# A memory-augmented attention chain with swapped weights: weight loads issued at even steps of TensorE's program, and stores, x and left-row transfers placed behind them in SyncE's program

## The chip, the cores and the metric

The kernel is written for one Trainium2 chip and uses one of its cores. A core has TensorE (matrix products, shown as PE, its weight loads as PEld), VectorE (DVE), ScalarE (ACT), GpSimd (POOL) and SyncE (SP), and 16 DMA engines that move data between HBM and the on-chip memory. Each engine runs its own list of instructions in order and waits on semaphores. The metric is the device time of one execution in microseconds; three runs of the kernel before took 1645.34, 1648.09 and 1649.2 us (median 1648.09).

## The reference

A sequence of 2048 tokens of width 640 goes through attention in 64 segments of 32 tokens, one after the other, because each segment hands 8 memory rows to the next. Beside it the same tokens go through a gated feed-forward block, and a gate mixes the two. Cut to what matters:

```python
for s in range(n_seg):                      # 64 segments of 32 tokens
    h = concatenate([mem, x[s]])            # 8 memory rows + 32 tokens
    q, k, v = h @ Wq, h @ Wk, h @ Wv        # 640 -> 32 heads of 192, each
    p = softmax(where(mask, q @ k.T * scale, -1e9))
    o = (p @ v) @ Wo                        # 32*192 -> 640
    mem = o[:8]
    outs.append(o[8:])
a = concatenate(outs)
b = (gelu(x @ w_gate) * (x @ w_up)) @ w_down
out = g * a + (1 - g) * b                   # g = sigmoid((x * gate_w).sum(-1))
```

## The kernel before, in words

The feed-forward block runs first and leaves its result in a scratch tensor in HBM. Then come the 64 segments. All lists of instructions are recorded by a small scheduler: `add` notes for each operation which earlier operations it must wait for (by the memory regions that it reads and writes), and each engine runs its operations in the order in which they were recorded. DMAs of this stage are all issued by SyncE.

**Segments.** A segment's work on TensorE is written out by hand in `PROG` (or `PROG1`, `PROG3`, by q = s mod 4): `("g", i, k)` is step k of 5 of group i of the projections, `sc`, `ex`, `pt`, `pv` are scores, softmax, transposition and product with V for one octet (a quarter of the heads), `wo` the output projection, `lf` and `vb` projections of "left rows". Of a segment's 32 tokens the first 24 and the 8 memory rows go through the projections as one block of 32; the last 8 tokens of four segments in a row make a block of their own, the left rows, which is projected ahead of time (a group of four segments has the number g).

**Weights.** The projection weights stand in pieces of 384 KB (a matrix, an octet, a step k; 60 pieces) and 480 KB (16 pieces of Wo). They don't all fit on the chip, so 16 slots hold two pieces in turn. Even segments use the octets in the order 0, 1, 2, 3, odd ones in the order 3, 2, 1, 0. A segment uses the pieces of its first octet in these slots and then loads over them those of its last octet, which it uses near its end and the next segment uses at its beginning. Of these 16 loads 12 are for Q, K and V (two of Q, five of K, five of V), 3 for Wo, and one piece of Q has a path of its own (L1459 copies it out of the way first).

**Where loads are issued.** After each item of the program `swap_loads` looks at the pieces that the item has used (`done_keys`) and records at once the load of the partner of each (`load_piece`, L635). The load waits for the last TensorE operation that reads the old piece. As the pieces of the first octet are used by groups 0 and 1, the 12 loads stand in SyncE's list close behind each other, and the three of Wo behind the two halves of `("wo", 0)`.

**What else SyncE issues in a segment.** `out_store` (L1029) writes the finished rows of the segment before, `x_load` (L743) reads the tokens of the next one, `bz_load` (L1018) reads the feed-forward result into the buffer that `out_store` has emptied, `stg_load` (L1005) reads projected left rows. In segments with q = 0, `outl_store` (L1072) writes the left rows of the group before in two parcels of four small DMAs; in segments with q = 2, `bzl_load` (L1024) reads the feed-forward result for left rows, also in two parcels of four. The scheduler holds that a later write of the same output rows waits for the earlier one: the four rows of segments that `outl_store` covers lie within those of `out_store`, the last of which is the one that is issued in the same segment (q = 0). `bz_load` waits for the landing of `out_store`, since it fills the same buffer. At the end of a segment POOL scales that buffer (L1085, `mix`) and DVE adds the attention's result (L1087).

**Places.** Before the change, `out_store` stands behind `("g", 0, 3)` where q = 0 and behind `("g", 1, 4)` otherwise, `x_load` behind `("g", 1, 4)`; the first parcel of `outl_store` and `bzl_load` stands behind `("g", 1, 4)`, the second behind `("pv", 2)`.

Of the kernel before, what the change touches and what calls it, by code (L numbers as in the profile page):

```python
# [238 lines left out]
def _build(nc, A_x, A_mem0, A_Wq, A_Wk, A_Wv, A_Wo, seg_len, w_gate, w_up, w_down,  # L239
# [9 lines left out]
    KT = Dm // 128  # L249
# [3 lines left out]
    NOCT = NT // 4  # L253
# [20 lines left out]
    S_ = _Sched(nc)  # L274
# [354 lines left out]
    later = []  # L629

    loaded = {}

    def load_piece(key, name):
        loaded[slot_id[key]] = key
# [3 lines left out]
    def piece(seg, key):  # L638
        order = orders[seg % 4]
        oi = last_req.get(seg, -1) + 1  # L640
        assert order[oi] == key, "pieces must be consumed in order"
        last_req[seg] = oi
        if seg == 0 and key in tmp_off:
            return left_piece(key)
        if seg and key == (EM, octet(seg, 0), EK):
            return None, None
        done_keys.append(key)
        return piece_view(key, res_off[key]), r_res[key]

    def swap_loads(seg, item):  # L650
        if item[:2] == ("g", 0) and EK <= item[2] < KT - 1:
            later.extend(key for key in done_keys if key[0] == 1)
            done_keys[:] = [key for key in done_keys if key[0] != 1]
        elif later:
            done_keys[:] = sorted(done_keys + later, key=lambda key: key[:1] + key[2:])
            del later[:]
        for key in done_keys:
            other = swap_in.get(key)
            if other is None or (other in partner) == (seg % 2 == 0):
                continue  # L660
            load_piece(other, "swap s%d" % seg)
        del done_keys[:]

    def left_piece(key):
        if key in tmp_off:
# [796 lines left out]
    def segment(s):  # L1462
        g, q = s // 4, s % 4
        post = []
        n_wo, nqkv = n_wos[q], nqkvs[q]
        for n, item in enumerate(PROGS[q]):
            kind, i = item[0], item[1]
            if kind == "g":
                proj(s, item)
                if item == ("g", 0, EK):  # L1470
                    left_fill(s, 0)
                    if s:
                        S_.add("pool", lambda e: e.memset(Qz[0:64], 0.0), writes=[r_Qz], name="Qz zero s%d" % s)
                        S_.add("pool", lambda e: e.memset(pl_sb, 0.0), writes=[r_p], name="pl zero s%d" % s)
                ki = [j for m, j in GROUPS[i] if m == 1 and item[2] == KT - 1]
                kind, i = ("k", ki[0]) if ki else ("", 0)
            elif kind == "tq":
                row_transp(s, 0, i)
            elif kind == "tk":
                row_transp(s, 1, i)  # L1480
            elif kind == "sc":
                scores(s, i)
            elif kind == "ex":
                softmax(s, i)
            elif kind == "pt":
                p_transp(s, i)
            elif kind == "pv":
                pv_oct(s, i)
                if i == NOCT - 1 and q < 3:
                    half_sums(OB, "s%d" % s)  # L1490
            elif kind == "lf":
                if i == q and unit(s, item[2]):
                    if item[3] == 0:
                        for m in range(2):
                            lb[item[2], m] = misc_bank(s)
                    for m in range(2):
                        LBK[m] = lb[item[2], m]
                    left_mm(*unit(s, item[2]), item[3], unit_piece)
            elif kind == "vb":
                if q == 3 and g + 1 < NG:  # L1500
                    if i == 0:
                        lb["v"] = misc_bank(s)
                    vl_mm(s + 1, i)
            elif kind == "le":
                if i == q and unit(s, item[2]):
                    if n > n_wo:
                        post.append(item[2:])
                    else:
                        left_evac(s, *item[2:])
            else:  # L1510
                if q == 3:
                    wo_both(s, item)
                else:
                    wo_part(s, item)
            swap_loads(s, item)
            if item == ("g", 0, KT - 2):
                for x in to_store:
                    left_store(*x)
                del to_store[:]
                if s and q == 0:  # L1520
                    out_store(s - 1)
            if item == ("g", 1, KT - 1):
                if q:
                    out_store(s - 1)
                if s + 1 < NSEG:
                    x_load(s + 1)
            if item == ("sc", NOCT - 1) and s + 1 < NSEG:
                ek_copy(s, (0, 1))
                ek_copy(s, (2,))
            if item == ("pv", NOCT - 1) and q == 3 and s + 1 < NSEG:  # L1530
                mix_left_b(g)
            if item == ("pv", NOCT - 1) and q == 1:
                stg_load(s + 1, 1)
            if n == ek_at[q]:
                if s + 1 < NSEG:
                    if q != 1:
                        stg_load(s + 1, 0)
                    key = (EM, octet(s, NOCT - 1), EK)
                    load_piece(swap_in[key], "swap s%d" % s)
                    stg_load(s + 1, int(q != 1))  # L1540
            if s == 0 and item == ("g", 0, KT - 1):
                load_residents(3, lambda key: key[0] < 3 and on_tmp(key))
            if s == 0 and item == late_at:
                load_residents(3, lambda key: key[0] == 3)
            if item == ("wo", 0, 1):
                for x in mid_later:
                    mid_store(x)
                del mid_later[:]
                if s + 1 < NSEG:
                    bz_load(s)  # L1550
                else:
                    end_load()
                    end_gates()
                if q == 1 and g + 2 < NG:
                    xl_load(g + 2)
            if item in (("g", 1, KT - 1), ("pv", NOCT - 2)):
                js = (0, 1) if item[0] == "g" else (2, 3)
                if q == 0 and g > 0:
                    outl_store(g - 1, js)
                if q == 2 and g + 1 < NG:  # L1560
                    bzl_load(g, js)
            if n == nqkv and s + 1 < NSEG:
                x_copy(s + 1)
        if s + 1 == NSEG:
            end_store()
            return
        kv = [x.rearrange("p (c k) -> p c k", k=KT) for x in (Zt, ps[:, OB2, SC:512], zsum)]
        if q == 3:
            for j in (0, 2, 1, 3):
                dst, src = Zt[32 * j:32 * j + 32], ps[64 * (j // 2):64 * (j // 2) + 32, LB, DJ * (j % 2):DJ * (j % 2 + 1)]  # L1570
                if j < 2:
                    S_.add("dve", lambda e, dst=dst, src=src: e.tensor_copy(out=dst, in_=src),
                           reads=[r_lbq[0]], writes=[r_PTq[j]], name="Zq evac s%d" % s)
                else:
                    S_.add("act", lambda e, dst=dst, src=src: e.activation(out=dst, in_=src, func=ACTF.Copy),
                           reads=[r_lbq[2]], writes=[r_PTq[j]], name="Zq evac s%d" % s)
        for i in range(2):
            ka, kb = KA[i], KA[i + 1]
            if q < 3:
                S_.add("dve", lambda e, ka=ka, kb=kb: e.tensor_tensor(  # L1580
                    out=kv[0][:, :, ka:kb], in0=kv[1][:, :, ka:kb], in1=kv[2][:, :, ka:kb], op=ALU.add),
                    reads=[r_ps[OB2], r_zp[0]], writes=[r_Z[i]] + ([r_PT] if i == 0 else []), name="Z%s evac s%d" % ("a" if i == 0 else "", s))
            S_.add("dve", lambda e, ka=ka, kb=kb: e.transpose(  # L1583
                out=XB4[:, :, ka:kb, XA:L].rearrange("p g k i -> p k g i"), in_=kv[0][:, :, ka:kb].rearrange("p c k -> p k c")),
                reads=[r_Z[i]] + (r_PTq if q == 3 else []), writes=[r_Hm[i], r_Qm, r_Ql], name="Tm%d s%d" % (i, s))
        mix(s)
        if q == 3:
            left_sums(g)
        if "v" in lb:
            tick[0] += 1  # L1590
            misc[lb["v"]] = tick[0]
            vl_evac(s + 1, octet(s + 1, 0), lb.pop("v"), "act")
        for i in post:
            left_evac(s, *i)
# [82 lines left out]
```

## Time and profile before

| | |
|---|---|
| device time, median of 3 runs (lowest to highest) | 1648.09 us (1645.34 to 1649.2) |
| profiled execution, first to last instruction (its span, the only time that it has) | 2114.2 us |
| TensorE clock granted in it | 0.654 of full speed |
| bytes moved by DMA | 499.28 MB, mean 236 GB/s |
| busy: TensorE, VectorE, ScalarE, GpSimd | 99%, 48%, 38%, 26% of the span |
| swapped weights: loads of L635 by SyncE, Wk, Wv, Wq, Wo | 335, 335, 209, 205 |

The profile is one execution, taken apart from the timed runs, and it is longer than they are. Its rows give an engine, a line of the program, an operation, what it writes and reads, how many and how long; "out<-in" names tensors (`arena` is the on-chip memory, `ps` the accumulators). In a time line a row is a run of equal instructions: start, length, count. SyncE's rows (SPq) are the issuing of DMAs, not their transfer; the time to landing is given apart, where the trace has it.

### The profile page before, as it was taken

What the parts mean: (1) busy time and instruction counts of PE and PEld (TensorE: products, weight loads), DVE (VectorE), ACT (ScalarE), POOL (GpSimd) and SP (SyncE); (2) the same over time, 40 slices, a digit from 0 to 9 for tenths busy, and PEclk for the clock granted to TensorE, in tenths of its full rate; (3) what the DMA queues carried; (4) which work ended last, traced back from release to release, by engine and by line L of the source; (5) the groups of instructions that cost most, each with busy time, mean ns of one, the idle gap of its engine ahead of it and who ended that gap; (6) DMA issues with size and microseconds to landing.
All of it is one profiled execution on the core that took longest, in us unless ns stands there. A gap on an engine that the chain in (4) does not pass through costs nothing.

```text
span 2114.2 us, 75845 instructions
## 1 busy us (share of the span) xinstructions
PE 2098.0 (99%) x37107; PEld 958.1 (45%) x28147; DVE 1005.8 (48%) x3039; ACT 792.9 (38%) x1890; POOL 553.3 (26%) x1625
## 2 busy tenths in 40 slices
PE   9999999999999999999999999999999999999997
PEld 3444344444444444444444444444444444444444
DVE  4233254554545454545545454545455454545453
ACT  1111244343434343444434343434444343434342
POOL 1000023232232223232222323232322223222332
PEclk6666666666666666666666666666666666666666
DMA  9612577776768777677767677776777676777775
GB/s 319 182 33 57 184 268 260 248 270 232 253 219 275 244 258 241 227 255 254 274 233 249 221 268 249 255 251 225 248 256 270 239 258 212 261 256 249 254 264 174
DMA packets 275415, 499.28 MB, mean 236 GB/s; under 512 B 121119, under 2 KB 136327, under 8 KB 275079
## 3 DMA queue, kind: packets, MB, share of 16 engines
q1 hardware_dynamic: 271000, 491.30, 68.8%
q8 instruction: 255, 4.18, 0.8%
q10 hardware_dynamic: 4079, 3.14, 0.5%
q14 instruction: 81, 0.66, 0.1%
HBM read 473.25 MB, written 21.09 MB: 234 GB/s over the span
## 4 chain that ended last, share of the span: by engine, by line
PE 99%; DMA 0%; DVE 0%; SPq 0%; POOL 0%; ACT 0%; issue 0%; ACTq 0%; POOLq 0%; DVEq 0%
PE ps L226 26%; PE ps L1138 25%; PE ps L1338 9%; PE ps L1383 8%; PE ps L1282 4%; PE ps L930 4%; PE ps L839 4%; PE ps L836 4%; PE ps L862 3%; PE ps L1364 3%; PE ps L1187 2%; PE ps L1284 2%; PE ps L234 1%; PE ps L1195 1%; PE ps L971 1%; PE ps L1254 1%
## 5 line engine op out<-in xcount | busy, mean ns | idle before, releaser
L226 PE MATMUL ps<-arena 128*32 128x384 bf16 x8960 | 887.8, 430 | 0.4 <-ACT arena L1159 0.4
L1138 PE MATMUL ps<-arena 128*32 128x384 bf16 x8640 | 857.5, 420 | 2.0 <-DVE arena L1583 2.0
L1138 PEld LDWEIGHTS ps<-arena 128*32 128x32 bf16 x8640 | 303.3, 117 | 525.3 <-issue 379.7
L1176 DVE STREAM_TRANSPOSE arena<-arena 128x384 bf16<-128x384 bf16 x512 | 276.5, 562 | 144.1 <-ACT arena L1159 144.1
L1159 ACT ACTIVATE arena<-ps 128x384 bf16<-128x384 f32 x512 | 230.0, 491 | 160.1 <-PE ps L1138 160.1
L1214 DVE TENSOR_REDUCE arena<-ps 104x4 f32<-104x160 f32 x256 | 83.0, 324 | 340.2 <-PE ps L1202 340.2
L1338 PE MATMUL ps<-arena 128*32 128x320 bf16 x3456 | 241.0, 404 | 0.0
L1012 POOL COPY arena<-arena 128x96 bf16<-128x96 bf16 x256 | 70.2, 274 | 475.3 <-PE ps L1202 311.4
L1267 ACT ACTIVATE arena<-ps 128x448 bf16<-128x448 f32 x192 | 104.4, 544 | 237.7 <-PE ps L1254 233.3
L1179 POOL COPY arena<-arena 64x160 bf16<-64x160 bf16 x256 | 81.9, 320 | 385.5 <-DVE arena L1176 384.3
L1162 ACT ACTIVATE arena<-ps 128x384 bf16<-128x384 f32 x256 | 125.2, 489 | 128.1 <-PE ps L1138 127.5
L1383 PE MATMUL ps<-arena 128*64 128x320 bf16 x1536 | 169.6, 387 | 0.0
L1226 ACT ACTIVATE ps<-ps 104x160 f32<-104x160 f32 x256 | 74.8, 292 | 239.5 <-DVE ps L1216 239.5
L1320 ACT ACTIVATE arena<-ps 128x480 bf16<-128x480 f32 x192 | 109.5, 570 | 93.8 <-PE ps L1284 85.7
L930 PE MATMUL ps<-arena 128*32 128x384 bf16 x1280 | 142.5, 408 | 0.0
L1338 PEld LDWEIGHTS ps<-arena 128*32 128x32 bf16 x3456 | 113.3, 129 | 56.9 <-ACT arena L1261 18.1
L1282 PE MATMUL ps<-arena 128*64 128x160 bf16 x1536 | 135.2, 263 | 0.0
L1284 PE MATMUL ps<-arena 128*64 128x64 bf16 x1536 | 128.6, 225 | 0.0
L1228 DVE TENSOR_REDUCE arena<-ps 104x4 f32<-104x160 f32 x256 | 81.8, 319 | 88.4 <-ACT ps L1226 87.4
L1383 PEld LDWEIGHTS ps<-arena 128*64 128x64 bf16 x1536 | 93.2, 127 | 49.4 <-issue 9.6
L1282 PEld LDWEIGHTS ps<-arena 128*64 128x64 bf16 x1536 | 94.1, 126 | 42.8 <-ACT arena L1159 23.0
L1411 ACT ACTIVATE arena<-ps 128x384 bf16<-128x384 f32 x120 | 57.3, 491 | 123.9 <-DVE arena L1580 74.0
(102 smaller groups left out, 2518.2 us busy)
## 6 DMA issues: line engine op xcount, KB each, us to landing
arena<-in_A_Wk_dram SPq DMA_DIRECT2D x335, 384.0 KB, 5.8
arena<-in_A_Wv_dram SPq DMA_DIRECT2D x335, 384.0 KB, 8.4
arena<-in_A_Wo_dram SPq DMA_DIRECT2D x205, 480.0 KB, 4.3
arena<-in_A_Wq_dram SPq DMA_DIRECT2D x209, 384.0 KB, 4.8
arena<-left_qk_scratch SPq DMA_DIRECT2D x126, 96.0 KB, 3.9
left_qk_scratch<-arena SPq DMA_DIRECT2D x49, 192.0 KB, 4.6
left_qk_scratch<-arena SPq DMA_DIRECT2D x30, 96.0 KB, 3.7
ffn_b_scratch<-arena ACTq DMA_DIRECT2D x16, 160.0 KB, 2.3
```

What stands on the lines that cost most here:

```text
L226: return e.add_instruction(mybir.InstMatmult(name=nm, start_tensor_calc=like["start"], stop_tensor_calc=stop, tile_size=(128, 32), tile_po ...
L930: fns.append(lambda e, outp=outp, rhs=rhs, j=j: e.matmul(outp, lhs, rhs, start=(k == 0), stop=(k == KT - 1), tile_position=(0, 32 * j)))
L1138: fns.append(lambda e, outp=outp, rhs=rhs, j=j: e.matmul(outp, lhs, rhs, start=(k == 0), stop=(k == KT - 1), tile_position=(0, 32 * j)))
L1159: S_.add("act", lambda e, m=m, bk=bk: e.activation(out=rows_sb[m], in_=ps[:, bk, 0:384], func=ACTF.Copy), reads=[r_ps[bk]], writes=[r_rows ...
L1162: S_.add("act", lambda e, i=i, bk=bk: e.activation(out=v_sb[i % NVB].rearrange("p (c n) -> p c n", c=3), in_=ps[:, bk, 0:384].rearrange("p ...
L1176: S_.add("dve", lambda e: e.transpose(out=dst[:, :, 0:L], in_=rows_sb[m].rearrange("p (c r) -> p c r", r=L)), reads=[r_rows[m]], writes=[r ...
L1267: S_.add("act", lambda e: e.activation(out=PT, in_=ps[:, bank, 0:PTW + 128], func=ACTF.Copy), reads=[r_ps[bank]], writes=[r_PT], name="pT ...
L1282: return [lambda e: e.matmul(full, v[:, e0:e0 + 64], PTm[:, i], start=True, stop=False, tile_position=(0, 64 * i), skip_group_check=True), ...
L1284: lambda e: e.matmul(part, vl[:, e0:e0 + 64], PTl[:, i], start=False, stop=True, tile_position=(0, 64 * i), skip_group_check=True)]
L1320: S_.add("act", lambda e: e.activation(out=apx(u[:, 0, 0, :], [[rs, na], [3 * rs, 4], [1, R]]), in_=ps[:, A, 0:na * W].rearrange("p (c t r ...
L1338: fns.append(lambda e, i=i, t=t, j=j, gv=gv: e.matmul(ps[32 * j:32 * j + 32, bank, 0:2 * DJ].rearrange("p (h n) -> p h n", h=2), lhs2[i], ...
L1383: S_.add("pe", [lambda e, i=i, g_=g_, c=c, p=p, u=u: e.matmul(ps[64 * i:64 * i + 64, LB, 0:2 * DJ], u[:, c, :], g_[:, c, 2 * DJ * i:2 * DJ ...
```

## The change

The diff moves no operation of TensorE, VectorE, ScalarE or GpSimd; what differs is the place of SyncE's DMAs in its list and what the swapped loads wait for.

- A piece whose partner is to be loaded goes into a list `pend`. A clock adds up a duration for each item of TensorE's program (`item_ns`: 162 ns for a projection piece, 405 for an item of `wo`, and so on), and a load is taken from the list at most every 900 of these nanoseconds (`next_load`), or when its piece is needed.
- Each such load also waits for the TensorE operation that was recorded last when it was taken from the list.
- `out_store` of the segment before and `x_load` of the next stand behind `("sc", 2)`, for every q.
- The first parcel of `outl_store` (q = 0) and of `bzl_load` (q = 2) stands behind `("g", 4, 4)`.

```diff
+    pend, clock, SPACE = [], [0, 0], 900
...
     def piece(seg, key):
...
+        while key in pend:
+            next_load(seg)
         done_keys.append(key)
...
     def swap_loads(seg, item):
...
-            load_piece(other, "swap s%d" % seg)
+            pend.append(other)
         del done_keys[:]
+        clock[0] += item_ns(seg, item)
+        while pend and clock[0] >= clock[1]:
+            next_load(seg)
+
+    def next_load(seg):
+        load_piece(pend.pop(0), "swap s%d" % seg)
+        S_.streams["sp"][-1].deps.add(S_.streams["pe"][-1])
+        clock[1] = max(clock[1], clock[0] - SPACE) + SPACE
+
+    def item_ns(seg, item):
+        q = seg % 4
+        if item[0] == "g":
+            return 162 * (len(GROUPS[item[1]]) + int(q == 0 and any(m == 2 and i for m, i in GROUPS[item[1]])))
+        if item[0] == "lf":
+            return 325 if item[1] == q else 0
+        if item[0] == "wo":
+            return 810 if q == 3 else 405
+        return {"sc": 470, "pv": 500, "pt": 100, "vb": 162}.get(item[0], 0)
...
-                if s and q == 0:
-                    out_store(s - 1)
-            if item == ("g", 1, KT - 1):
-                if q:
+            if item == ("sc", 2):
+                if s:
                     out_store(s - 1)
                 if s + 1 < NSEG:
                     x_load(s + 1)
...
-            if item in (("g", 1, KT - 1), ("pv", NOCT - 2)):
+            if item in (("g", 4, KT - 1), ("pv", NOCT - 2)):
```

In SyncE's list of a segment with q = 0 the order around the three Wo pieces was: 12 pieces of Q, K and V with `out_store` after the third, `x_load`, four `outl_store`, three pieces of Wo, `bz_load`, `stg_load`, the single piece of Q, `stg_load`, four `outl_store`. After the change it is: 12 pieces, `out_store`, `x_load`, two pieces of Wo, four `outl_store`, the third piece of Wo, `bz_load`, and then as before. With q = 2 the same holds for `bzl_load`. With q = 1 and 3 the order is unchanged but for the places in time.

## The prediction

> **What bounds the kernel now.** I read the head of the page, the cores' clock and TensorE's own waits first.
>
> ```profile
> span 2114.2 us, 75845 instructions
> PE 2098.0 (99%) x37107; PEld 958.1 (45%) x28147; DVE 1005.8 (48%) x3039; ACT 792.9 (38%) x1890; POOL 553.3 (26%) x1625
> ...
> core 0: 2114.2 us, clock 0.654
> ...
> PE ps L836 <- DMA arena<-in_B_w_gate_dram: 0.4, 1, 0.4
> ```
>
> TensorE is busy for 99% of the span, and in the whole list of its waits a DMA stands once, with 0.4 us, for the first weights of the feed-forward block. In this execution the kernel is bound by TensorE alone, at a granted clock of 0.654, and no swapped piece is ever late.
>
> The timed runs are something else: their median, 1648.09 us, is 0.78 of the span. TensorE's 2098.0 us at 0.654 are 1372 us at full clock, so the timed runs had a granted clock between 1372/1648 = 0.83 (if TensorE never waits) and 1 (if 276 us are waits, 4.3 us for each of 64 segments). The trace cannot say where between. I therefore do the sum twice: at the trace's own times, and for the timed runs, where I let all marks of TensorE come at 0.78 of their distance from the segment's start, while DMA transfers and SyncE's issuing keep their lengths.
>
> [...]
>
> Then the DMA side: two stretches of a segment with q = 0 (the burst of 12 loads, the rest), a stretch within a burst, times to landing by issue, those of all L635, the ns (min/median/max) that issuing a piece of Wo takes, and one of SyncE's own waits.
>
> ```profile
> 1182.80:1199.10 16.30, 16.30 (x320) 5.57 (x198) 8.28 (x25) 6.11 (x16) 3.24 (x12) 0.65 0.85 298
> 1199.10:1212.30 13.20, 13.20 (x298) 7.86 (x270) 6.83 (x24) 4.75 (x12) 4.68 (x12) 0.65 0.51 164
> ...
> 1015.00:1023.00 8.00, 8.00 (x158) 2.31 (x82) 4.95 (x16) 4.09 (x10) 1.92 (x7) 0.65 1.04 413
> ...
> arena<-in_A_Wv_dram SPq DMA_DIRECT2D x335, 384.0 KB, 8.4
> arena<-in_A_Wo_dram SPq DMA_DIRECT2D x205, 480.0 KB, 4.3
> arena<-left_qk_scratch SPq DMA_DIRECT2D x126, 96.0 KB, 3.9
> arena<-x_scratch SPq DMA_DIRECT2D x63, 30.0 KB, 8.7
> ...
> DMA to landing us min/median/max: 3.1/5.7/13.6
> ...
> L635 SPq DMA_DIRECT2D arena<-in_A_Wo_dram x205: 327/334/1707, 181.8 to 2091.1; - x103
> ...
> SPq L1005 <- DMA left_qk_scratch<-arena: 20.8, 15, 3.0
> ```
>
> The last two columns are the DMA engines' share and GB/s: in the burst the engines are full (413 GB/s, 0.95 us for each 384 KB piece), afterwards half idle. What is issued behind the burst lands 8.4 to 8.7 us later, what is issued elsewhere after 3.1 to 4.3. The last row shows that SyncE does stand still for a landing where one DMA must follow another: 15 times, 20.8 us in all, up to 3.0.
>
> **The change, part by part.** SyncE's time line in segment 32 (q = 0; it starts at 1182.30), and the marks on TensorE and POOL that matter:
>
> ```profile
> 1182.79 1.02 SPq L635 DMA_DIRECT2D arena<-in_A_Wk_dram  x2
> ...
> 1187.65 4.17 SPq L635 DMA_DIRECT2D arena<-in_A_Wv_dram  x5
> 1191.86 0.43 SPq L743 DMA_DIRECT2D arena<-x_scratch  x1
> 1192.34 2.46 SPq L1072 DMA_DIRECT2D out_dram<-arena  x4
> 1200.35 3.75 SPq L635 DMA_DIRECT2D arena<-in_A_Wo_dram  x3
> 1204.14 0.59 SPq L1018 DMA_DIRECT2D arena<-ffn_b_scratch  x1
> ...
> 1182.30 0.45 PE L1138 MATMUL ps<-arena 128*32 128x384 bf16 x4
> ...
> 1196.01 0.71 PE L1138 MATMUL ps<-arena 128*32 128x384 bf16 x8
> ...
> 1206.58 0.71 PE L1138 MATMUL ps<-arena 128*32 128x384 bf16 x8
> ...
> 1210.17 1.42 PE L1364 MATMUL ps<-arena 128*32 128x160 bf16 x48
> ...
> 1210.79 0.69 POOL L1085 TENSOR_SCALAR arena<-arena 128x160 bf16<-128x160 bf16 x1 [0.17 <-POOL arena L1080]
> 1212.79 0.33 POOL L1012 COPY arena<-arena 128x96 bf16<-128x96 bf16 x1 [1.31 <-DVE arena L1583]
> ```
>
> *Pacing of the 12 pieces.* Nothing is added on any computing engine. The last piece of V, issued about 1191.4 today, is now released by the left-row product of group 3, step 1 (the row at 1196.01), so at about 1196.4. It lands between 1199.5 (3.1 us, alone) and 1204.8 (8.4 us, behind a queue) and is used at 1206.58: covered. Timed, it is released at 14.1 x 0.78 = 11.0 us and used at 24.3 x 0.78 = 18.9; between it lands at 14.1 at the earliest and, if the DMA works through the 12 no faster than in the burst's 16.3 us, from 0.4 on, at 16.7. The cover is at least 2.2 us: cost 0. What hides it is TensorE's work up to group 5; if it were gone, every segment would pay.
>
> *`out_store` and `x_load` behind the pieces.* `x_load` stands behind the last V piece today as well; its copy comes after the last use of V, so the cover above holds: 0. `out_store` alone costs nothing either. It matters through what waits for its landing.
>
> *Left-row stores (q = 0, 15 segments: group 0 has none).* They must wait for `out_store`, and now stand between the second and the third Wo piece, so behind a waiting SyncE are queued the third Wo piece, `bz_load`, two `stg_load` and the single Q piece. At the trace's clock: `out_store` is issued at about 1196.9, pieces come 1.2 us apart against 0.95 us of DMA each, so no queue; by the nearest rows it lands at 1200.0 (3.1) to 1201.2 (4.3). SyncE is through with two Wo pieces at 1201.0, the four stores take 2.46 us, 1203.5 to 1203.7; the third Wo piece is released by TensorE at 1203.77 anyway (the Wo row's end less one issue of 0.33). Sum: nothing.
>
> Timed: two Wo pieces are out at 18.05 x 0.78 + 0.67 = 14.8. `out_store` is issued at 11.4 and lands at 14.5 (3.1) or, where the DMA is as full as in the burst, at 16.7. The stores end at 17.2 to 19.2, where the third Wo piece goes out today at 21.47 x 0.78 = 16.7. It lands 4.3 later, 21.5 to 23.5; its last quarter of the 48 products begins at 28.9 x 0.78 = 22.5: a stall of 0 to 1.0. `bz_load` follows by 0.33 and lands 3.9 later (as L1005, the nearest in kind), 21.5 to 23.4; POOL wants it at 28.5 x 0.78 = 22.2: 0 to 1.2 late. What is late next is POOL's copy for the next segment's scores (L1012, 30.5 x 0.78 = 23.8). The two stalls overlap: 0 to 1.2 us a segment. I take 0.7, nearer the full queue: the two stretches above hold 16.3 x 298 + 13.2 x 164 = 7000 KB, 17 us at 413 GB/s, in a timed segment of 23.4. 15 x 0.7 = 10.5 us (0 to 18).
>
> *Left-row loads (q = 2, 15 segments)*, with no landing to wait for, move to the same place; segment 26 starts at 1009.4:
>
> ```profile
> 1009.39 0.62 PE L1138 MATMUL ps<-arena 128*32 128x384 bf16 x4
> ...
> 1018.50 2.71 SPq L1024 DMA_DIRECT2D arena<-ffn_b_scratch  x4
> 1026.17 2.81 SPq L635 DMA_DIRECT2D arena<-in_A_Wo_dram  x3
> ...
> 1033.88 1.35 PE L1364 MATMUL ps<-arena 128*32 128x160 bf16 x46
> ```
>
> Here: 1026.17 + 0.67 + 2.71 = 1029.6 instead of 1028.65 for the third Wo piece, landing 1033.9, used at 1034.9: covered by 1.0. Timed: 16.5 instead of 15.0, landing 20.8, used at 25.5 x 0.78 = 19.9: 0 to 0.9 late, since today's landing at 19.3 leaves 0.6. I take 0.3, nearer to the covered case that the row shows: 4.5 us (0 to 13.5).
>
> **Sum.** Against the profiled execution: 2114.2 + 0. For the timed runs: 1648.1 + 10.5 + 4.5 = 1663 us, its own range 1648 to 1680.
>
> **Rivals.** *The covers hold as in the trace*, 1648: the change then does nothing that shows. For it speaks that the first sum is 0; against it, that timed marks are 22% closer.
>
> *Faster.* With the loads spread, small transfers need not lie 8.7 us behind a burst but land after 3.8 to 4.3, and waits for them that only timed runs have go away. [...] Place: the swapped Wo pieces, `bz_load` and `stg_load` at a segment's end. If 0.35 us of the 4.3 unexplained ones are of this kind, 64 x 0.35 = 22 us: 1626. Against it: those transfers stand outside the burst today as well and land in 3.9 to 4.3, and TensorE's list has no wait for them.
>
> *Pieces late in every segment.* It decides from the point where a piece takes more than (18.9 - 0.4 - 3.1)/12 = 1.28 us of DMA instead of 0.95; at 1.33, 0.6 x 64 = 38 us: 1686.
>
> **How the numbers follow.** Stalls behind SyncE 0.57, covers hold 0.15, faster 0.18, late pieces 0.10. The likeliest gives 1663. A measurement of this kernel can tell about 0.2%, 3.3 us, from no change. Slower is the first case but for 0.02 of it, and the last: 0.65; same 0.15 + 0.02 = 0.17; faster 0.18. The range reaches half way into both outer cases, 1636 to 1688.
>
> **What would show it.** In SyncE's waits, L1072 waiting for the landing of the output store, some 15 times, none with q = 2; the third Wo issued after the four stores, not at TensorE's mark; V pieces landing in 4 to 6 us instead of 8.4; at a granted clock of 0.65 a span within 2 us of 2114, at a higher one TensorE waits at L1364 for Wo, or POOL at L1085 for the feed-forward rows, with q = 0 alone. Waits at L1138 or L226 for swapped pieces would speak for late pieces; q = 1 and 3 segments shorter than 0.78 of these, for the faster case. The prediction is wrong if the timed runs are at 1645 or below.

## The result, and the profile after

The changed kernel took 1665.41 us (median of 4 runs, 1663.36 to 1670.37) against 1648.64 us for the kernel before (median of 4, 1645.34 to 1652.01): a ratio of 1.0098, 95% interval 1.0073 to 1.0122. It is slower, by 16.8 us, where 1663 was forecast.

The profiled execution of before had a granted clock of 0.654; that of the changed kernel had 0.996. So that the two can be laid side by side, the kernel before was profiled once more, and this execution had 0.998. It is the one used below. In the changed kernel's program L1159 is L1138 of before, L1385 is L1364, L1093 is L1072, L1039 is L1018, L636 is L635.

The head of the page, the DMA queue and the median times to landing of the changed kernel:

```profile
span 1665.3 us, 75844 instructions
PE 1568.6 (94%) x37107; PEld 770.4 (46%) x28147; DVE 998.3 (60%) x3039; ACT 785.7 (47%) x1890; POOL 552.6 (33%) x1625
q1 hardware_dynamic: 271000, 491.30, 84.7%
...
arena<-in_A_Wv_dram SPq DMA_DIRECT2D x335, 384.0 KB, 6.5
arena<-in_A_Wo_dram SPq DMA_DIRECT2D x205, 480.0 KB, 6.4
...
arena<-x_scratch SPq DMA_DIRECT2D x63, 30.0 KB, 5.9
```

The same rows of the kernel before, in its second profile:

```profile
span 1642.3 us, 75828 instructions
PE 1562.6 (95%) x37090; PEld 772.6 (47%) x28147; DVE 998.1 (61%) x3039; ACT 784.4 (48%) x1890; POOL 552.6 (34%) x1625
q1 hardware_dynamic: 271000, 491.30, 85.3%
...
arena<-in_A_Wv_dram SPq DMA_DIRECT2D x335, 384.0 KB, 8.5
arena<-in_A_Wo_dram SPq DMA_DIRECT2D x205, 480.0 KB, 6.0
...
arena<-x_scratch SPq DMA_DIRECT2D x63, 30.0 KB, 8.6
```

At granted clocks of 0.996 and 0.998 one queue keeps the 16 DMA engines busy for 85% of the span in both kernels. V pieces and x now land sooner after they are issued (6.5 for 8.5 us, 5.9 for 8.6), and yet the kernel is slower: they are issued later, and counted from the start of the segment the last V piece lands 0.30 us later, not earlier (table below).

Where the time went stands in TensorE's waits (us in total, times, longest), first of the changed kernel:

```profile
PE ps L1385 <- DMA arena<-in_A_Wo_dram: 15.2, 27, 1.3
PE ps L1159 <- DMA arena<-in_A_Wv_dram: 9.2, 19, 1.9
PE ps L1159 <- DMA arena<-in_A_Wk_dram: 4.3, 6, 1.3
PE ps L1404 <- DMA arena<-in_A_Wo_dram: 1.5, 4, 0.5
...
SPq L1093 <- DMA out_dram<-arena: 27.1, 15, 2.9
```

and of the kernel before:

```profile
PE ps L1364 <- DMA arena<-in_A_Wo_dram: 4.1, 14, 0.8
PE ps L1138 <- DMA arena<-in_A_Wv_dram: 3.5, 10, 0.5
PE ps L1138 <- DMA arena<-in_A_Wk_dram: 1.4, 1, 1.4
PE ps L1383 <- DMA arena<-in_A_Wo_dram: 1.0, 4, 0.4
```

TensorE waits 30.2 us for swapped pieces instead of 10.0, which is 20.2 of the 23.0 us between the two profiled executions (1667.01 and 1644.05). Idle stretches that the trace puts down to no cause ("issue") come on top of these, 19.9 us after and 20.8 us before. The last row of the changed kernel is the wait that was predicted for SyncE, 15 times. The kernel before has no such row, but SyncE stands still for the landing of the output store there too: at `bz_load` (L1018), 58.9 us in 34 times, which is 39.1 us in 25 times in the changed kernel.

For all kernels below I took three things from the trace: the length of a segment by q (from the end of VectorE's last transpose of one segment, L1602, before L1583, to that of the next; the mean of 14 segments), the same waits of TensorE's products for in_A_Wq, Wk, Wv and Wo added up (idle stretches of more than 0.15 us), and by how much later than in the kernel before the last V piece lands (counted from the segment's start, mean of the four q). These come from the one profiled execution, whose time stands beside them; the ratio is that of all timed runs.

```
kernel                  ratio (95% interval)     profiled  waits   V late   q=0   q=1   q=2   q=3
before, again           -                        1644.05   10.0     0      23.46 22.87 22.21 22.33
changed                 1.0098 (1.0073..1.0122)  1667.01   30.2    +0.30   23.90 23.21 22.38 22.70
e1 store to q=1         1.0100 (1.0069..1.0132)  1661.49   27.2    +0.21   23.17 23.56 22.44 22.54
e2 moves only           1.0006 (0.9986..1.0025)  1648.54   15.7    -0.01   23.82 22.72 22.22 22.36
e3 pacing only          1.0315 (1.0280..1.0351)  1706.49   59.8    +1.31   25.25 23.02 24.01 22.26
e4 marks, no spacing    1.0076 (1.0050..1.0101)  1661.23   27.3    +0.32   23.81 23.05 22.49 22.57
e5 spacing, first free  1.0073 (1.0045..1.0102)  1656.28   23.0    +0.12   23.80 23.09 22.36 22.32
e6 before, half pieces  0.9782 (0.9754..0.9810)  1614.22    4.3    -1.40   22.58 22.41 21.51 22.12
e7 changed, half pieces 0.9806 (0.9771..0.9842)  1619.46   15.6    -1.20   22.56 22.37 21.80 22.14
e8 first piece, end     1.0036 (1.0013..1.0059)  1652.35   18.0    +0.21   23.64 22.76 22.47 22.40
   of its step
e9 first piece, end     1.0106 (1.0075..1.0137)  1661.85   24.3    +0.55   23.58 22.79 22.30 23.21
   of the next step
e10 before, store q=1   1.0023 (1.0002..1.0044)  1658.12   22.9    +0.27   23.51 23.01 22.87 22.31
e11 moves, store q=1    1.0033 (1.0012..1.0053)  1646.08   14.6    +0.05   23.30 22.84 22.46 22.25
```

One profiled execution is a thin basis for 0.1 us a segment: 29 timed runs of the kernel before lie between 1641.72 and 1658.34 us, which is 0.26 us for each of 63 segments. Some of the profiled executions are also quick ones of their kernel: that of e1 took 1661.49 us of a median of 1669.14, that of e5 1656.28 of 1663.24, that of e11 1646.08 of 1654.81. Verdicts below rest on the ratios; the columns by q say where to look.

### The profile page after: what moved, and what is told of

Its sections match the earlier page's. It is cut to its first block, busy times and chain, and to the rows that moved or that the text cites. A ratio compares the mean times of both kernels' runs of the same rounds, so it can differ in the third digit from the quotient of the medians.

```text
span 1665.3 us, 75844 instructions
## 1 busy us (share of the span) xinstructions
PE 1568.6 (94%) x37107; PEld 770.4 (46%) x28147; DVE 998.3 (60%) x3039; ACT 785.7 (47%) x1890; POOL 552.6 (33%) x1625
## 5 line engine op out<-in xcount | busy, mean ns | idle before, releaser
L1159 PE MATMUL ps<-arena 128*32 128x384 bf16 x8640 | 641.6, 329 | 21.6 <-DMA arena<-in_A_Wv_dram 9.2
L226 PE MATMUL ps<-arena 128*32 128x384 bf16 x8960 | 645.1, 327 | 3.7 <-ACT arena L1180 1.0
L1159 PEld LDWEIGHTS ps<-arena 128*32 128x32 bf16 x8640 | 226.0, 96 | 400.7 <-issue 265.4
L1197 DVE STREAM_TRANSPOSE arena<-arena 128x384 bf16<-128x384 bf16 x512 | 272.9, 559 | 71.8 <-ACT arena L1180 70.7
L1359 PE MATMUL ps<-arena 128*32 128x320 bf16 x3456 | 183.7, 300 | 10.9 <-issue 5.9
L1033 POOL COPY arena<-arena 128x96 bf16<-128x96 bf16 x256 | 70.2, 274 | 249.6 <-PE ps L1223 174.7
L1404 PE MATMUL ps<-arena 128*64 128x320 bf16 x1536 | 122.6, 304 | 1.7 <-DMA arena<-in_A_Wo_dram 1.5
L1303 PE MATMUL ps<-arena 128*64 128x160 bf16 x1536 | 117.6, 240 | 6.9 <-issue 3.5
L1359 PEld LDWEIGHTS ps<-arena 128*32 128x32 bf16 x3456 | 88.2, 96 | 56.1 <-ACT arena L1282 19.8
L951 PE MATMUL ps<-arena 128*32 128x384 bf16 x1280 | 107.6, 328 | 0.7 <-issue 0.7
L1305 PE MATMUL ps<-arena 128*64 128x64 bf16 x1536 | 103.7, 193 | 1.9 <-issue 1.9
L1349 POOL COPY arena<-arena 128x96 bf16<-128x96 bf16 x192 | 51.7, 269 | 160.2 <-ACT arena L1331 93.2
L1303 PEld LDWEIGHTS ps<-arena 128*64 128x64 bf16 x1536 | 81.4, 109 | 40.1 <-ACT arena L1183 14.4
```

The costliest lines, as they stand in the source:

```text
L226: return e.add_instruction(mybir.InstMatmult(name=nm, start_tensor_calc=like["start"], stop_tensor_calc=stop, tile_size=(128, 32), tile_po ...
L951: fns.append(lambda e, outp=outp, rhs=rhs, j=j: e.matmul(outp, lhs, rhs, start=(k == 0), stop=(k == KT - 1), tile_position=(0, 32 * j)))
L1159: fns.append(lambda e, outp=outp, rhs=rhs, j=j: e.matmul(outp, lhs, rhs, start=(k == 0), stop=(k == KT - 1), tile_position=(0, 32 * j)))
L1197: S_.add("dve", lambda e: e.transpose(out=dst[:, :, 0:L], in_=rows_sb[m].rearrange("p (c r) -> p c r", r=L)), reads=[r_rows[m]], writes=[r ...
L1303: return [lambda e: e.matmul(full, v[:, e0:e0 + 64], PTm[:, i], start=True, stop=False, tile_position=(0, 64 * i), skip_group_check=True), ...
L1305: lambda e: e.matmul(part, vl[:, e0:e0 + 64], PTl[:, i], start=False, stop=True, tile_position=(0, 64 * i), skip_group_check=True)]
```

## The experiments

**Which half of the change costs: four runs.** Theory A was the prediction's (SyncE held up by the left-row stores), theory B its rival of late pieces. First the kernel before, for its profile:

> The kernel before once more, for a profile to lay beside that of the changed kernel, whose granted clock was 0.996. Theory A (the loss is made where SyncE, with q = 0, waits 1.8 us for the output store's landing and issues four left-row stores ahead of the third Wo piece): segments with q = 0 are 0.7 to 1.0 us shorter here than in the changed kernel, those with q = 2 0.2 to 0.4 us, those with q = 1 and 3 the same within 0.1. Theory B (the pacing lets the swapped pieces come late in every segment): all four kinds are shorter here, each by about 0.27 us (17 us over 63 segments). If the clock is 0.65 again, nothing of this can be read and only the time counts, 1645 to 1652.

Its segments are shorter than the changed kernel's for every q, by 0.44, 0.34, 0.17 and 0.37 us: not A's pattern.

Then the changed kernel with half of the stores moved away from the place that A blames (the added lines stand behind `x_load`):

```diff
+                if q == 1 and g > 0:
+                    outl_store(g - 1, (0, 1))
...
-                if q == 0 and g > 0:
+                if q == 0 and g > 0 and item[0] == "pv":
                     outl_store(g - 1, js)
```

> The changed kernel, but the first two quarters of the left-row stores are issued one segment later (q = 1, behind x_load), when the output store on which they depend landed long ago: neither a landing wait nor four issues stand ahead of the third Wo piece with q = 0. Theory A: some 15 x 0.7 to 1.0 us come back, 1650 to 1657, ratio to the kernel before 1.001 to 1.005, SyncE's 15 waits for the output store go away, q = 0 segments shorter by 0.7 to 1.0 us. Theory B: nothing comes back, 1.008 to 1.012. In between, if the four issues cost q = 1 as much as the wait cost q = 0.

The wait of SyncE for the output store at the left-row stores went away, and the traced segments with q = 0 came down from 23.90 to 23.17 us. Nothing came back in the time all the same: 1.0100. Segments with q = 1, where the four issues now stand between V and Wo, went from 23.21 to 23.56. In TensorE's waits the cost has moved with the stores: its products wait for Wo pieces 0.8 us in all with q = 0 instead of 8.2 in the changed kernel, and 6.2 with q = 1 instead of 1.4. So the run moves the cost of the stores to another segment and does not take it away.

The moves without the pacing:

```diff
-            pend.append(other)
+            load_piece(other, "swap s%d" % seg)
```

> The changed kernel without the pacing: the swapped pieces are issued at once where they were issued in the kernel before, and only the moves of output store, x and left-row transfers remain. Theory A: most of the loss stays, 1.005 to 1.009 (1656 to 1663), all of it in q = 0 and a little in q = 2. Theory B: nothing of it stays, 0.998 to 1.002.

1.0006: the moves alone cost 1 us (-2.3 to 4.1). Theory A is not the main cause, unless the moves cost more beside the pacing than alone. Its mechanism is there nonetheless; in SyncE's time line of segment 32 (q = 0, from 907.64) the stores stand ahead of the third Wo piece:

```profile
914.12 0.59 SPq L1050 DMA_DIRECT2D out_dram<-arena  x1
914.75 0.56 SPq L764 DMA_DIRECT2D arena<-x_scratch  x1
920.62 1.74 SPq L636 DMA_DIRECT2D arena<-in_A_Wo_dram  x2
923.76 2.42 SPq L1093 DMA_DIRECT2D out_dram<-arena  x4
926.22 0.41 SPq L636 DMA_DIRECT2D arena<-in_A_Wo_dram  x1
926.67 0.59 SPq L1039 DMA_DIRECT2D arena<-ffn_b_scratch  x1
```

The output store, issued 6.5 us into the segment, lets the left-row stores go only at 16.1: it lies in the queue behind the V pieces, the last of which lands at 16.04 on average. The third Wo piece goes out at 18.06 instead of 15.95 (mean with q = 0), but lands only 0.6 later, 21.86 instead of 21.24, since in the kernel before it stood behind two other Wo pieces in the DMA queue anyway (the second of which lands at 19.5). That is what became of a delay of 2.1 us.

The pacing without the moves, `out_store`, `x_load` and the left rows where they stood:

```diff
+                if s and q == 0:
+                    out_store(s - 1)
+            if item == ("g", 1, KT - 1):
+                if q:
                     out_store(s - 1)
...
-            if item in (("g", 4, KT - 1), ("pv", NOCT - 2)):
+            if item in (("g", 1, KT - 1), ("pv", NOCT - 2)):
```

> The changed kernel without the moves: the swapped pieces are paced, output store, x and left-row transfers stand where they stood. Theory A as it stands: no loss, 0.998 to 1.002. Theory B: the whole loss, 1.008 to 1.012, in all four kinds of segments. A third, C (any four DMAs of the left rows among the paced pieces hold the pieces behind them back, wherever they stand): a loss of 1.005 to 1.013 in q = 0 and q = 2 alone, now with waits of TensorE at L1159 for pieces of V.

1.0315, more than any theory gave. C's pattern fits: q = 0 and q = 2 pay 1.8 us each, the other two 0.15 and -0.07. In segment 32 (from 936.02) the paced pieces now stand behind the stores, as a list that runs in order has it:

```profile
939.27 1.20 SPq L636 DMA_DIRECT2D arena<-in_A_Wk_dram  x2
940.52 0.43 SPq L764 DMA_DIRECT2D arena<-x_scratch  x1
942.28 2.42 SPq L1093 DMA_DIRECT2D out_dram<-arena  x4
944.74 0.41 SPq L636 DMA_DIRECT2D arena<-in_A_Wk_dram  x1
945.20 2.59 SPq L636 DMA_DIRECT2D arena<-in_A_Wv_dram  x5
```

The last piece of K goes out 8.7 us into the segment, where the changed kernel issues it at 5.5; the last piece of V lands at 19.12 us (mean, q = 0; 16.52 in the changed kernel, 16.28 in the kernel before), and TensorE waits for V:

```profile
PE ps L1159 <- DMA arena<-in_A_Wv_dram: 46.9, 62, 3.2
```

So pacing needs the moves, and the moves alone do nothing that can be measured in the time. The run also speaks against a simple form of theory B: with q = 1 and q = 3 it has the marks and the spacing of the changed kernel, its last V piece lands 0.37 and 0.10 us late there, and yet these segments pay nearly nothing.

**How the pacing costs: marks or spacing.** A paced piece waits for two things: for the end of the step of TensorE's program in which its turn comes (the mark), and for 900 ns since the piece before (the spacing). The changed kernel with 0 in place of 900 has the marks alone:

```diff
-    pend, clock, SPACE = [], [0, 0], 900
+    pend, clock, SPACE = [], [0, 0], 0
```

> Theory A is gone (the moves alone gave 1.0006), and theory B splits in two: the swapped pieces land late in all four kinds of segments because (B1) the first pieces of a segment now wait for the end of the whole step of TensorE's program, which starts the DMA's 16 pieces 0.15 to 0.35 us later, or (B2) the 900 ns between the pieces leaves the DMA engines short of work in the middle of the segment. This is the changed kernel with 0 in place of 900: every piece still waits for the end of its step, and none is held back further. B1: most of the loss stays, 1.004 to 1.009. B2: the time of the moves alone, 0.999 to 1.003.

1.0076: most of the loss is there. The first piece of a segment is issued 0.17 us later than in the kernel before and lands 0.24 later, the last piece of V 0.32 (means over q).

The other way round, the first pieces free and the others spaced:

```diff
             pend.append(other)
+            fresh.add(other)
...
             next_load(seg)
+        fresh.clear()
...
+        late = pend[0] not in fresh
         load_piece(pend.pop(0), "swap s%d" % seg)
-        S_.streams["sp"][-1].deps.add(S_.streams["pe"][-1])
+        if late:
+            S_.streams["sp"][-1].deps.add(S_.streams["pe"][-1])
```

> The changed kernel with its 900 ns, but a piece that goes out in the step that frees it no longer waits for the end of that step (only the held-back ones wait for TensorE's mark). B1: the first piece of a segment lands 0.15 to 0.35 us earlier and most of the loss goes, 1.001 to 1.005. B2: the loss stays, 1.007 to 1.012.

1.0073, the loss that B2 expected, but the interval, 1.0045 to 1.0102, reaches into what B1 expected (1.001 to 1.005). Nor is this a clean run of the spacing. The held-back pieces still have their marks, and with q = 1 the first piece is not early at all: it goes out 0.28 us into the segment (mean of 14; -0.01 in the kernel before). In six of these 14 segments it follows directly on the four left-row stores that SyncE still has to issue from the segment before, as in segment 33 (from 932.36; L1098 and L637 are L1093 and L636 here):

```profile
930.03 2.42 SPq L1098 DMA_DIRECT2D out_dram<-arena  x4
932.50 0.88 SPq L637 DMA_DIRECT2D arena<-in_A_Wk_dram  x2
```

The changed kernel has this in eight of the 14, the moves alone in four, the kernel before in none. The last V piece is late by 0.07, 0.33, 0.11 and -0.03 us (q = 0 to 3) in this trace: where the first piece is free, the spacing hardly delays it. With 1.0076, 1.0073 and 1.0098 for marks, spacing and both, whose intervals overlap, the runs do not divide the loss between the two; they show only that neither, left out, takes the loss away. Other spacings were not tried.

**Is the DMA what passes the delay on?** Both kernels with every swapped piece halved:

```diff
-        S_.add("sp", lambda e: e.dma_start(piece_view(key, res_off[key]), piece_src(key)), writes=[r_res[key]],
+        n = 64 if name[:4] == "swap" else 128
+        S_.add("sp", lambda e: e.dma_start(piece_view(key, res_off[key])[0:n], piece_src(key)[0:n]), writes=[r_res[key]],
```

> The kernel before with every swapped piece halved: only its first 64 of 128 partitions are loaded, the other half of each weight stays that of the piece that lay there before. Both B1 and B2 need a DMA that is full for most of a segment. If it is so, TensorE's waits for in_A_Wv, in_A_Wk and in_A_Wo go away (10 us of its matmuls in the kernel before) and with them 10 to 40 us: 1610 to 1640. If the DMA has room already, 1645 to 1650, same as before.

> The changed kernel with every swapped piece halved in the same way. B (a full DMA turns the later start of pieces into waits of TensorE): the difference between the two kernels shrinks to that of the moves, 0 to 4 us against the halved kernel before. If the difference stays at 15 us or more, the loss has nothing to do with how full the DMA is.

0.9782 and 0.9806, medians 1614.14 and 1618.54: some 36 us go (31 to 41, by the ratio of 0.9782), and of the change's 16.8 us 4.4 are left, near the 0 to 4 that B expected, though the two intervals overlap. The first piece of a segment still goes out 0.22 us later in the changed kernel of this pair (0.24 for 0.03), but here that costs little. The lever is a smaller one than I had meant. The queue's row of the halved kernel before:

```profile
q1 hardware_dynamic: 205976, 282.11, 75.7%
```

Bytes fall by 43%, the share of time only from 85.3% to 75.7%, and pieces land 0.92 us apart instead of 1.02 (means from the seventh to the twelfth). Half pieces, whose last V lands 1.40 us earlier, are thus worth some 36 us in the kernel before, 0.57 us a segment: TensorE at 95% busy does depend on the DMA stream. Its named waits for swapped pieces are the smaller part of that. Of the 29.8 us between the two profiled executions (1644.05 and 1614.22) they make up 5.7; idle stretches without a named cause fall from 20.8 to 6.0 us, and the busy time falls by 7.4 (1562.6 to 1555.2). Why these two fall is not shown.

**A dose test of the late start.** The kernel before, nothing moved, nothing spaced; only the first piece of each segment waits, and eleven queue behind it:

```diff
             load_piece(other, "swap s%d" % seg)
+            if seg != lead[0]:
+                lead[0] = seg
+                S_.streams["sp"][-1].deps.add(S_.streams["pe"][-1])
```

> The kernel before, but the first swapped piece of each segment waits for the end of the step of TensorE's program that frees it (in the traces so far about 0.15 us later); all other pieces go out at once behind it, nothing is moved. The 16 pieces land one after the other, about 1.0 us each for 384 KB, so a late first piece should make all of them late. B1: the last V piece and the three Wo pieces land 0.1 to 0.2 us later in all four kinds of segments, 1.003 to 1.007. If only the later pieces' marks or the 900 ns matter: 0.998 to 1.002.

The same, but the pieces freed by `("g", 0, 0)` are held and issued behind the next step:

```diff
-            load_piece(other, "swap s%d" % seg)
+            held.append(other)
         del done_keys[:]
+        if item == ("g", 0, 0):
+            return
+        for other in held:
+            load_piece(other, "swap s%d" % seg)
...
+        del held[:]
```

> The same with a dose three times as large: the first piece waits for the end of TensorE's next step, 0.4 to 0.6 us later than in the kernel before. B1: three times the loss of the run before, with the landings shifted by the whole 0.4 to 0.6 us and the segments by at least half of it: 1.012 to 1.022 (63 x 0.3 to 0.6 us). If the queue takes the shift up, 0.998 to 1.003.

The first piece was issued 0.13 and 0.46 us later, the last V piece landed 0.21 and 0.55 later, and the ratios are 1.0036 and 1.0106, about 1 to 3 as the doses are, though the larger came out below its expected range: 17.5 us over 63 segments are 0.28 each, half of the shift. In single kinds of segments the traces are uneven: with the small dose the last V piece is late by 0.36, -0.02, 0.47 and 0.03 us (q = 0 to 3), not in all four kinds as expected, and with the large dose q = 3 pays 0.88 and q = 1 nothing. That a late first piece makes the kernel slower is shown. The first piece of the changed kernel is 0.16 us late, near the smaller dose, and by that it would account for some 6 (2 to 10) of the 16.8 us; this is an estimate. What the marks on the later pieces add (1.0076 with all of them) wasn't tried by itself.

**A version that beats both?** The kernel before, and the moves alone, with the first half of the stores at the end of the segment with q = 1, where SyncE has nothing else to issue:

```diff
+            if item == ("pv", NOCT - 2) and q < 2 and g > 0:
+                outl_store(g - 1, (2, 3) if q == 0 else (0, 1))
```

> A try for a version that beats both: the kernel before, but the first two quarters of the left-row stores go out one segment later, at the end of the one with q = 1 (behind the single Q piece, where SyncE has nothing to issue), so that SyncE never waits for the output store's landing. In the run that moved them into q = 1 of the changed kernel, segments with q = 0 were 23.17 us against 23.46 in the kernel before. If that holds here and q = 1 pays nothing: 15 x 0.3 us, 0.996 to 0.999. If the stores at the end of q = 1 hold the first pieces of q = 2 back: 1.000 to 1.004.

> The moves without the pacing (1.0006), and the same two quarters of the stores at the end of q = 1. The part of theory A that is left says that q = 0, 23.82 us with the moves alone, comes down by 0.36 us or more, SyncE's waits for the output store go away and the third Wo piece goes out near 16 us instead of 18.1: 0.995 to 0.999. If q = 0 is held by something else: 0.999 to 1.003.

1.0023 and 1.0033: neither. With e11 SyncE's wait at the left-row stores is gone and q = 0 is 0.52 us shorter than with the moves alone (23.30 for 23.82). But in both kernels SyncE is through with the four issues and a `stg_load` behind them only 0.38 and 0.35 us into the next segment, q = 2 (mean of 14), and the first piece of that segment goes out 0.4 us later (0.43 and 0.44 instead of 0.03). That is a late first piece, as in the dose test. Of the kernels that load all pieces, the kernel before is not beaten.

## Why the prediction came out, point by point

**The time was right, its sum was not.** 1663 was made of 15 us for the moves and 0 for the pacing. Measured are 1 us for the moves alone and the rest, 1.0098 / 1.0006 = 1.0092 or 15 us, for the pacing on top of them. Two errors of one size and opposite sign met: that the sum came out at 1663 is luck. How the 15 us divide between the pacing itself and what it adds to the cost of the moves is open (see the left-row stores below).

**The step that failed: "Pacing of the 12 pieces", cost 0.** It checked the cover of one piece, the last of V, in one kind of segment, q = 0. This piece was covered, by 1.57 us on average where at least 2.2 was computed. But of the last V pieces it is the best covered. From the landings and the first products that use each piece, in the changed kernel:

```
piece            cover in us, mean of 14 segments (times below 0.25)
                 q=0        q=1        q=2         q=3
second of V      1.11 (2)   0.54 (6)   0.06 (13)   2.76 (0)
last of V        1.57 (0)   1.00 (1)   0.12 (12)   0.35 (5)
third of Wo      -          0.22 (9)   -           0.08 (14)
```

The second V piece with q = 2 has no cover at all (the landing's record is missing for the third Wo piece with q = 0 and 2). One such segment of the changed kernel, 34 (from 959.74), in TensorE's time line; the brackets are idle time and what ended it:

```profile
971.76 0.98 PE L1159 MATMUL ps<-arena 128*32 128x384 bf16 x19
...
973.16 0.50 PE L1159 MATMUL ps<-arena 128*32 128x384 bf16 x5 [0.42 <-DMA arena<-in_A_Wv_dram]
...
974.14 0.35 PE L1159 MATMUL ps<-arena 128*32 128x384 bf16 x4 [0.47 <-DMA arena<-in_A_Wv_dram]
```

The same segment of the kernel before (from 949.55) runs 28 products from the same point, 12.0 us into the segment, without a stop of more than 0.15 us:

```profile
961.58 1.57 PE L1138 MATMUL ps<-arena 128*32 128x384 bf16 x28
```

This pair of segments is one of the clearer ones. At a granted clock of 0.998 the kernel before has no cover there either. In its second profile, up to the first product that waits for the piece, the second V piece with q = 2 has 0.07 us on average (below 0.25 in all 14), the last V piece with q = 2 has 0.21 (in 10), and the third Wo piece with q = 3 has 0.10 (in 13). Ahead of the second V piece with q = 2, TensorE stands still in 8 of 14 segments, for 0.18 us on average over all 14; in the changed kernel in 11 of 14, for 0.28. In the profile that the prediction had, at 0.654, the same piece had 3.7 us of cover. So the change did not use up a cover that was there: at 0.998 these pieces had 0.07 to 0.21 us of cover before it, so that a later landing of them could be paid for at once.

**Bound by TensorE alone, at a granted clock of 0.654.** It was so in that execution only. With the clock at 0.998 TensorE is busy for 1562.6 us in the kernel before, not for the 1372 that 2098.0 us at 0.654 were scaled to, and waits 10.0 us for pieces. Nor do all marks come at 0.78 of their time: the segments shrank to 0.78, 0.78, 0.83 and 0.74 (23.46 of 30.12 for q = 0, and so on); q = 2, least of all, is the one whose V pieces have no cover. The thirteen other profiled executions told of here had a granted clock of 0.987 to 0.998; what lowered the first one to 0.654 is not shown.

**`out_store` and `x_load`: 0.** Agrees with 1.0006 for all moves.

**Left-row stores, 15 x 0.7 = 10.5 us.** The mechanism came as it was described: 15 waits of SyncE at L1093, the stores from 16.1 us on (segment 32 of the moves alone; the upper of the two cases computed, with a full queue, said 16.7), the third Wo piece at 18.1 with the moves alone and 18.6 in the changed kernel (17.2 to 19.2 computed). The size was off, because its landing was counted from its issue: it stands in a queue of Wo pieces, and 2.1 us of delay at SyncE are 0.6 at the landing. The trace with the moves alone has 0.36 us for q = 0, half of the 0.7, and the timed runs don't show it. Beside the pacing the stores weigh more in the traces: TensorE's waits for Wo pieces with q = 0 are 0.3 us in the kernel before, 4.6 with the moves alone and 8.2 in the changed kernel. So 7.9 of the 20.2 us that the waits grew by stand where the forecast had put 10.5. Whether the time falls by as much when the stores hold up nothing was not tried together with the pacing; e1 only moved them.

**Left-row loads, 15 x 0.3 = 4.5 us.** 0.01 us for q = 2 with the moves alone: nothing. TensorE's waits for Wo with q = 2 are 2.4 us in the kernel before, 4.1 with the moves alone and 5.3 in the changed kernel.

**The rivals.** The one that came is that of pieces late in every segment (chance 0.10), at 15 / 63 = 0.24 us instead of 0.6. Its condition, a piece that takes over 1.28 us of DMA, was wrong: pieces land 1.02 us apart before and 1.03 after. A stream that starts later is enough, as the dose test shows, though by its size it explains only a part of the 15 us. The signs named for the rival, waits at L1138 (L1159 in the changed kernel) for V, stood in the profile, and those named for the forecast, waits for Wo, stood there too, but not with q = 0 alone: 8.2 us there and 8.3 with the other three. "Faster by a lighter queue" had its premise, x landing after 5.9 us instead of 8.6, but in the second profile of the kernel before one wait alone is for such a load: POOL's at L811, once, for 43.4 us.

## What to carry to other kernels

A cover has to be computed for the piece that has least of it, in every kind of segment, and not for the last piece where the change is easiest to see. With one queue busy for 85% of the time, as in this kernel, the time from issue to landing was mostly queue (8.5 us for a V piece, 3.5 for the first piece of a segment): issuing later shortened it to 6.5 us and gained nothing, so landings are to be counted from the segment's start. What started this queue 0.13 and 0.46 us late cost 0.09 and 0.28 us a segment on average, unevenly over the four kinds. And when the profiled execution and the timed runs differ by a quarter, a second profile is worth more than a sum scaled to the other clock.

## What the runs showed of the hardware

Loading half of the partitions hardly shortened a load: 64 partitions, 197 kB, landed every 0.92 us (213 GB/s, the kernel before with half pieces), 128 partitions, 393 kB, every 1.02 us (385 GB/s, the kernel before in its second profile). The rate of the half pieces is 0.55 of the other; why is not shown. Whether halving the columns takes more load off the DMA was not tried.

A DMA that was issued late into this queue landed almost when it would have: 2.1 us later at SyncE, 0.6 us later in memory (third Wo piece, q = 0, with the moves alone). And the granted clock of this kernel and its variants, on one core, was 0.654 in one profiled execution and 0.987 to 0.998 in the other thirteen.
